# Turning the leading expert's second half of tokens ahead of the branch, with one raw buffer for the wide weights

## The chip, the cores and the metric

One core of one Trainium2 chip runs the whole kernel in one launch. The metric is the device time of that core in microseconds, as the median over several executions. Single executions of this kernel lie within about 0.3% of one another.

## The reference

Three stages follow one another; all is float32 but for `moe2`'s weights, which arrive as 64-bit floats.

```python
# attention: B, H, S, D = 4, 8, 768, 48, step by step over S
cur = einsum('bhd,bhe->bhde', u[None] * kt, vt)
y[:, :, t] = einsum('bhd,bhde->bhe', rt, state + cur)
state = wt[..., None] * state + einsum('bhd,bhe->bhde', kt, vt)
# x: 3072 tokens of 384; top-1 of 8 experts by cosine similarity
logits = xn @ en.T / tau
expert_idx = argmax(logits, axis=1); gate_w = softmax(logits)[chosen]
out[mask] = gate_w * (maximum(x[mask] @ w1[e], 0) @ w2[e])      # w1 384x1024, w2 1024x384
# wide stage on all tokens
h = maximum(maximum(x @ w1, x @ w2), x @ w3)                    # 384x768 each
return h @ w_out                                                # 768x384
```

## The kernel before

**Precision by halves.** Each matrix product of the last two stages is made of three single passes: a value is split into a high part (rounded to the matmul format) and a low part (the value minus the high one), and high x high, low x high and high x low are summed in PSUM. So every tile of weights or activations costs one copy (ScalarE, makes `hi`) and one subtraction (VectorE or GpSimd, makes `lo`).

**Attention and routing (span 0 to about 199 us).** The sequence is cut into 24 chunks of 128 tokens. Each chunk's outputs go to DRAM (`xs_d`), its logits feed the routing, which yields for each expert the list of its tokens. The expert with most tokens is known early. For it, called the leading expert or expert 0 here, the first 256 tokens (`EARLY`) are gathered, turned by TensorE (`early_x`, L851 on), split, and multiplied by `w1` in eight calls `early_h`, one per 128 columns of `w1`, all before the routing's last numbers are known. `early_lo` makes the low halves on VectorE. The gathers of its third and fourth quarter are issued on GpSimd after the last routing step, but nothing uses them before the branch.

**The branch.** The final counts of the experts choose one of three copies of the expert code, with different tile widths (`CAPS`). Every engine loads two numbers (`over`, L92) into registers and takes the branch (L100) for itself, when its own queue has come so far. In the profiled execution the copy with `CAPS[0]` runs, in which expert 0 has 432 columns.

**The experts (to about 419 us).** `experts()` (L1025 on) is a list written out by hand: all work is issued in program order (`manual_schedule`), and each engine takes its own instructions in that order, waiting by semaphores. It starts with `expert_x(0, 1)`, which turns and splits the gathered third and fourth quarter, and four matmuls on a constant tile (`IDLE[1]`), whose results nobody reads. Then 64 steps follow, eight per expert. Step s does `expert_h` of step s (9 matmuls), `expert_y` of step s-2 (9 matmuls), the copies and subtractions for coming weights, and their loads on SyncE. For expert 0, `expert_h` covers only columns 256 to 432.

**The wide weights.** 24 tiles of 128x384 of 64-bit words become hi and lo parts by integer steps on VectorE, in three stages (`wide_weights`, L940 on): stage 0 allocates a raw tile (`raw64`, two buffers) and issues its transfer of 384 KB on SyncE; stage 1 is four VectorE operations and the ScalarE copy that makes hi; stage 2 is four VectorE operations that make lo. In stage 1, the first operation (L960) reads the high words out of the raw tile, the fourth (L964) reads them again. In stage 2, L970 writes a scratch tile `t2`, L971 reads the low words and `t2`, L972 reads `t2` and writes lo. Tiles 0 to 17 are spread over the expert steps, tile i being loaded at step 2+3i, and its stages 1 and 2 done at steps 3+3i and 4+3i. Tiles 18 to 23, the six of `w_out`, are done in the wide stage.

**The wide stage (to the end).** Six blocks of 512 tokens; each has six `wide_h` (27 matmuls of 512 columns, then two maxima on VectorE, L999 and L1000, a copy on ScalarE and a subtraction on GpSimd, L1007) and four `wide_out` (18 matmuls each, L1017). The `wide_out` of block j run behind the first `wide_h` of block j+1. In block 0, each `wide_h` is followed in program order by stages 1 and 2 of one `w_out` tile, and the transfer of the tile after next; after the second `wide_h` VectorE also splits the next block's activations (`split_y`). The first `wide_out` needs all six `w_out` tiles, the last of them for its last three matmuls.

Of the kernel before, what the change touches and what calls it, by code (L numbers as in the profile page):

```python
# [20 lines left out]
DM = H * D  # L21
# [3 lines left out]
P = 128  # L25
# [11 lines left out]
IDLE = 4, 4  # L37
# [9 lines left out]
class Block:  # L47
# [6 lines left out]
    def run(self):  # L54
        tc, nc = self.tc, self.nc
        with ExitStack() as es:
# [8 lines left out]
                         for t in ("hw1", "lw1", "hw2", "lw2")}  # L65
            self.ring["raw"] = [ring.tile([P, 384], F32, name=f"raw_{i}") for i in range(RAW)]
# [45 lines left out]
    def attention(self):  # L112
# [3 lines left out]
        with ExitStack() as es:  # L116
# [97 lines left out]
            en = cp.tile([E, DM], F32, name="en")  # L214

            def setup2():
                ess = cp.tile([E, 1], F32, name="ess")
                enn = cp.tile([E, 1], F32, name="enn")
                act.activation(out=en, in_=emb, func=AF.Square, accum_out=ess)
# [6 lines left out]
                dve.tensor_scalar(out=en, in0=emb, scalar1=enn, scalar2=self.rtau[:E], op0=ALU.mult, op1=ALU.mult)  # L226
                dve.tensor_copy(enp[:, :, :D], en.rearrange("p (h d) -> p h d", h=H))
# [5 lines left out]
            def setup2b():  # L233
# [4 lines left out]
                for d in range(3):  # L238
                    pe.transpose(tq[:, d * E:(d + 1) * E], en[:, d * P:(d + 1) * P], ident[:E, :E])
# [357 lines left out]
            with tc.manual_schedule():  # L597
# [132 lines left out]
                for f in range(4, 8):  # L730
                    head(f)
                for n, op in enumerate(order()):
                    op()
                    if n == 0:
                        self.early_lo(2, early[2])
                offsets()
                for f in range(3, 8):
                    self.early_lo(f, early[f])

# [112 lines left out]
    def early_x(self, q, t):  # L852
# [4 lines left out]
        tv = t[:, :3 * P].rearrange("p (d t) -> p d t", d=3)  # L857
        two = lambda z: z.rearrange("p (d t) -> p d t", t=EARLY)
# [49 lines left out]
    def expert_h(self, e, f, c0=0):  # L908
        cap = self.caps[e]
        wh, wl = self.w1s[e, f]  # L910
        xh, xl = self.xT[e]
        t = self.ptile("h", 2)
        n = 0
        for a, b in ((wh, xh), (wl, xh), (wh, xl)):
            for d in range(3):
                self.pe.matmul(t[:, c0:cap], a[:, d, :], b[:, d, c0:], start=(n == 0), stop=(n == 8))  # L916
# [23 lines left out]
    def wide_weights(self, i, stage):  # L940
# [11 lines left out]
        if stage == 0:  # L952
            self.raws[0, i] = self.work.tile([P, 384], U64, tag="raw64", name="raw64")
# [13 lines left out]
        else:  # L967
            t1, t2 = self.wide, self.work.tile([P, 384], U32, tag="t1", name="t1", bufs=1)
# [57 lines left out]
    def experts(self):  # L1026
# [11 lines left out]
        with tc.manual_schedule():  # L1038
            self.dve.memset(self.gsort, 0.0)
            if early:  # L1040
                self.expert_x(0, 1)
                t = self.ptile("y", 3)
                for _ in range(IDLE[1]):
                    self.pe.matmul(t, self.warm[:, :P], self.warm, start=True, stop=True)
            else:
# [54 lines left out]
            for i in range(WIDE, WIDE + 2):  # L1100
                self.wide_weights(i, 0)
            k, pend = 0, None
            for j in range(6):
                hs, nxt = [], None
                for f in range(6):
# [6 lines left out]
                    if j == 0:  # L1112
                        for stage in 1, 2:
                            self.wide_weights(WIDE + f, stage)
                        if WIDE + f + 2 < 24:
                            self.wide_weights(WIDE + f + 2, 0)
# [164 lines left out]
```

## Time and profile before

| | |
|---|---|
| three timed runs | 735.00, 736.92, 737.33 us; median 736.92 |
| the profiled execution | 733.96 us; span of its instructions 732.2 us |
| busy: TensorE, VectorE, ScalarE, GpSimd | 708.7, 428.2, 306.8, 257.0 us |
| mean granted TensorE clock | 0.992 of full |
| DMA | 69.05 MB, 94 GB/s on average |

The span runs from the first to the last instruction of one execution; all times below are microseconds from its start. PE is TensorE's matmul side, PEld its weight loads, PEldq its sequencer; DVE is VectorE, ACT ScalarE, POOL GpSimd, SPq the queue of SyncE. `L916` is line 916 of the kernel before. Names of tiles stand without their numbers, `out<-in`; a name such as `mh` or `hw` can stand for another use of the same storage.

### The profile page before, as it was taken

The page shows a single profiled execution, that of the slowest core. Times are in us where ns is not written, and L with a number is a line of the kernel's source. Part 1 is how long each engine was busy: PE and PEld are TensorE (multiplying, and loading weights), DVE is VectorE, ACT ScalarE, POOL GpSimd, SP SyncE. Part 2 cuts the span into 40 slices and gives each one's busy share as a digit, 9 for nine tenths or more (in the row PEclk, how much of TensorE's full clock was granted, in tenths as well). Part 3 has the DMA queues.
Part 4 walks back from the last instruction along what each step waited for, and adds up shares of the span by engine and source line. Part 5 has one row for each costly group of instructions (what it writes and reads, how often), then busy time and mean ns, then how long its engine had stood idle before and what let it go on. Part 6 is the DMA issues. An engine that isn't in the chain of part 4 may idle for free.

```text
span 732.2 us, 13468 instructions
## 1 busy us (share of the span) xinstructions
PE 708.7 (97%) x4861; PEld 627.6 (86%) x4861; DVE 428.2 (58%) x938; ACT 306.8 (42%) x720; POOL 257.0 (35%) x271
## 2 busy tenths in 40 slices
PE   7999999999799999999999999999999999999994
PEld 4788888888789999999999988988988988889884
DVE  7889999998747986878788368431032031221110
ACT  4667666765445554555556322222121221221120
POOL 6857657476531401201100023343333333223122
PEclk9999999999999999999999999999999999999998
DMA  9997878753365537656554111000100100000001
GB/s 154 171 149 139 138 135 138 144 89 118 104 186 165 170 115 216 202 152 195 152 173 147 60 29 59 23 22 1 44 1 0 44 1 11 33 1 21 22 2 46
DMA packets 146444, 69.05 MB, mean 94 GB/s; under 512 B 104967, under 2 KB 140931, under 8 KB 146360
## 3 DMA queue, kind: packets, MB, share of 16 engines
q1 hardware_dynamic: 141752, 58.27, 35.1%
q0 software_dynamic: 4032, 9.74, 4.2%
q8 instruction: 42, 0.69, 0.4%
q14 instruction: 42, 0.34, 0.1%
q10 hardware_dynamic: 576, 0.01, 0.1%
HBM read 58.52 MB, written 9.48 MB: 93 GB/s over the span
## 4 chain that ended last, share of the span: by engine, by line
PE 85%; DVE 7%; issue 3%; DMA 2%; ACT 1%; POOL 1%; SPq 0%; POOLq 0%; DVEq 0%; ACTq 0%
PE psy L993 16%; PE psT L993 15%; PE psy L933 13%; PE psh L916 13%; PE psh L1017 9%; PE psT L275 4%; PE psA L356 3%; PE psM L426 3%; PE psY L417 3%; PE psY L410 2%; PE psM L384 1%; DMA out_dram<-raw,idx 1%; DVE es L337 1%; PE psM L294 1%; DVE gs L324 1%
## 5 line engine op out<-in xcount | busy, mean ns | idle before, releaser
L999 DVE TENSOR_TENSOR xg<-psT,xg 128x512 f32<-128x512 f32 x18 | 12.4, 690 | 112.8 <-PE psT L993 80.8
L827 DVE TENSOR_TENSOR lw<-raw,hw 128x384 fp32r<-128x384 f32 x120 | 62.3, 553 | 15.8 <-ACT hw L825 14.0
L825 ACT ACTIVATE hw<-raw 128x384 fp32r<-128x384 f32 x123 | 60.7, 524 | 17.7 <-ACT hw L825 10.2
L1007 POOL TENSOR_TENSOR lw<-xg,hw 128x512 fp32r<-128x512 f32 x24 | 31.5, 1311 | 100.4 <-ACT hw L1006 100.4
L841 POOL DMA_INDIRECT xg<-xs_d,idxs x25 | 26.8, 1073 | 111.0 <-PE psT L903 44.6
L1007 POOL TENSOR_TENSOR lh<-xg,hh 128x512 fp32r<-128x512 f32 x12 | 16.1, 1340 | 115.1 <-ACT hh L1006 115.1
L309 POOL TENSOR_SCALAR_AFFINE_SELECT AT<-c 128x1024 f32<-128x1024 f32 x24 | 38.9, 1619 | 49.0 <-ACT c L304 48.9
L1006 ACT ACTIVATE hw<-xg 128x512 fp32r<-128x512 f32 x24 | 15.2, 635 | 97.0 <-DVE xg L1000 97.0
L993 PE MATMUL psy<-yh,mh 128*128 128x512 f32 x162 | 46.7, 396 | 0.2 <-ACT ys L937 0.2
L993 PE MATMUL psy<-yl,mh 128*128 128x512 f32 x162 | 46.6, 395 | 0.0
L993 PE MATMUL psT<-yh,ml 128*128 128x512 f32 x162 | 46.6, 396 | 0.0
L993 PE MATMUL psy<-yh,ml 128*128 128x512 f32 x162 | 46.5, 396 | 0.0
L993 PE MATMUL psT<-yl,mh 128*128 128x512 f32 x162 | 46.5, 396 | 0.0
L993 PE MATMUL psT<-yh,mh 128*128 128x512 f32 x162 | 46.5, 395 | 0.0
L922 DVE SCALAR_TENSOR_TENSOR lh<-psh,hh 128x420 fp32r<-128x420 f32 (+6 forms) x56 | 31.4, 561 | 19.8 <-ACT hh L921 19.5
L916 PE MATMUL psh<-xh,hw 128*128 128x420 f32 (+7 forms) x177 | 42.0, 345 | 0.3 <-DVE lh L922 0.3
L916 PE MATMUL psh<-xh,lw 128*128 128x420 f32 (+7 forms) x183 | 42.0, 339 | 0.0
L1033 POOL DMA_INDIRECT out_dram<-raw,idx x24 | 23.7, 987 | 49.5 <-ACT raw L1023 32.5
L916 PE MATMUL psh<-xl,hw 128*128 128x420 f32 (+7 forms) x177 | 40.7, 337 | 0.0
L933 PE MATMUL psy<-hh,hw 128*128 128x420 f32 (+6 forms) x168 | 40.1, 344 | 0.0
L933 PE MATMUL psy<-lh,hw 128*128 128x420 f32 (+6 forms) x168 | 39.2, 341 | 0.0
L933 PE MATMUL psy<-hh,lw 128*128 128x420 f32 (+6 forms) x168 | 39.2, 341 | 0.0
(329 smaller groups left out, 1801.7 us busy)
## 6 DMA issues: line engine op xcount, KB each, us to landing
raw<-in_moe_w_dram SPq DMA_DIRECT2D x128, 192.0 KB
raw<-in_moe_w_dram SPq DMA_DIRECT2D x18, 384.0 KB
wb<-in_w_dram SPq DMA_DIRECT2D x24, 192.0 KB
kb<-in_k_dram SPq DMA_DIRECT2D x24, 192.0 KB
rb<-in_r_dram SPq DMA_DIRECT2D x24, 192.0 KB
vb<-in_v_dram SPq DMA_DIRECT2D x24, 192.0 KB
xs_d<-xt SPq DMA_DIRECT2D x24, 192.0 KB
raw<-in_moe_w_out_dram SPq DMA_DIRECT2D x6, 384.0 KB
```

What stands on the lines that cost most here:

```text
L275: pe.transpose(t[:112, p * P:(p + 1) * P], flat(src)[:, p * P:p * P + 112], ident)
L309: pool.affine_select(out=x["AT"].rearrange("s q p t -> s (q p) t"), in_=x["c"].rearrange("t q p -> t (q p)").unsqueeze(2).to_broadcast([P, ...
L825: self.act.activation(out=hi, in_=raw, func=AF.Copy)
L827: eng.tensor_tensor(out=lo, in0=raw, in1=hi.bitcast(F32), op=ALU.subtract)
L841: self.pool.indirect_dma_start(out=t[:n], out_offset=None, in_=self.xs_d[0:rows], in_offset=bass.IndirectOffsetOnAxis(ap=self.idxs[:n, 4 * ...
L916: self.pe.matmul(t[:, c0:cap], a[:, d, :], b[:, d, c0:], start=(n == 0), stop=(n == 8))
L922: self.dve.scalar_tensor_tensor(out=lo, in0=t[:, c0:cap], scalar=0.0, in1=hi.bitcast(F32), op0=ALU.max, op1=ALU.subtract)
L933: self.pe.matmul(self.yb[m][:, :cap], a[:, m, :], b, start=(f == 0 and n == 0), stop=(f == 7 and n == 2))
L993: self.pe.matmul(t, a[:, d, f * P:(f + 1) * P], b[:, d, :], start=(n == 0), stop=(n == 8))
L1007: self.pool.tensor_tensor(out=lo, in0=c2, in1=hi.bitcast(F32), op=ALU.subtract)
L1017: self.pe.matmul(t[:, :DM], a[:, c], b[:, f, :], start=(n == 0), stop=(n == 17))
L1033: self.pool.indirect_dma_start(out=self.out, out_offset=bass.IndirectOffsetOnAxis(ap=self.idx2[:, k:k + 1], axis=0), in_=o, in_offset=None ...
```

## The change

The third and fourth quarter of expert 0's tokens are turned by `early_x` behind the last `early_h`, still in the attention part, into a pair of tiles of their own (`x1`); ScalarE copies the high part at once, and VectorE's two subtractions come behind the last `early_lo`. `expert_h` of expert 0 reads that pair. `expert_x(0, 1)` and the four matmuls on the constant tile behind the branch go. The room for `x1` comes from three places: `raw64` has one buffer instead of two, stage 2 writes its scratch over the raw tile's high words, and a scratch tile of the setup goes (its two users write `emb` and another scratch tile). With one raw buffer a tile's transfer can only be issued once the tile before has gone through stage 2, and in block 0 of the wide stage the transfers are issued one tile ahead instead of two.

```diff
-IDLE = 4, 4
...
+            self.x1 = [ring.tile([P, 3, 512 - EARLY], F32R, name=f"x1{t}") for t in "hl"]
...
-            en = cp.tile([E, DM], F32, name="en")
...
-                act.activation(out=en, in_=emb, func=AF.Square, accum_out=ess)
+                act.activation(out=rp.tile([P, DM], BF16, tag="jq", name="jq")[:E], in_=emb, func=AF.Square, accum_out=ess)
...
                 for f in range(4, 8):
                     head(f)
+                rest = [self.early_x(q, bank("M", 3)) for q in (2, 3)]
                 for n, op in enumerate(order()):
                     op()
...
                 for f in range(3, 8):
                     self.early_lo(f, early[f])
+                for low in rest:
+                    low()
...
         tv = t[:, :3 * P].rearrange("p (d t) -> p d t", d=3)
+        if q > 1:
+            hi, lo = (z[:, :, (q - 2) * P:(q - 1) * P] for z in self.x1)
+            self.act.activation(out=hi, in_=tv, func=AF.Copy)
+            return lambda: self.dve.tensor_tensor(out=lo, in0=tv, in1=hi.bitcast(F32), op=ALU.subtract)
...
-        xh, xl = self.xT[e]
+        xh, xl = self.x1 if c0 else self.xT[e]
...
-                self.pe.matmul(t[:, c0:cap], a[:, d, :], b[:, d, c0:], start=(n == 0), stop=(n == 8))
+                self.pe.matmul(t[:, c0:cap], a[:, d, :], b[:, d, :cap - c0], start=(n == 0), stop=(n == 8))
...
-            self.raws[0, i] = self.work.tile([P, 384], U64, tag="raw64", name="raw64")
+            self.raws[0, i] = self.work.tile([P, 384], U64, tag="raw64", name="raw64", bufs=1)
...
-            t1, t2 = self.wide, self.work.tile([P, 384], U32, tag="t1", name="t1", bufs=1)
+            t1, t2 = self.wide, high
...
-            if early:
-                self.expert_x(0, 1)
-                t = self.ptile("y", 3)
-                for _ in range(IDLE[1]):
-                    self.pe.matmul(t, self.warm[:, :P], self.warm, start=True, stop=True)
-            else:
+            if not early:
...
-            for i in range(WIDE, WIDE + 2):
-                self.wide_weights(i, 0)
+            self.wide_weights(WIDE, 0)
...
-                        if WIDE + f + 2 < 24:
-                            self.wide_weights(WIDE + f + 2, 0)
+                        if WIDE + f + 1 < 24:
+                            self.wide_weights(WIDE + f + 1, 0)
```

## Rows read from the trace of the kernel before

**Rows 1.** The page's chain that ended last, share of the span by engine.

```profile
PE 85%; DVE 7%; issue 3%; DMA 2%; ACT 1%; POOL 1%; SPq 0%; POOLq 0%; DVEq 0%; ACTq 0%
```

**Rows 2.** Timeline of TensorE around the branch: start, us, operation, count, [idle before].

```profile
198.16 0.28 PE L876 MATMUL psT<-ml,mh 128*128 128x256 f32 x1
201.22 1.36 PE L903 MATMUL psT<-ident,hw 128*128 128x128 f32 x6 [2.78 <-issue]
202.51 1.89 PE L1044 MATMUL psy<-warm 128*128 128x512 bf16 x4
203.84 1.34 PE L916 MATMUL psh<-xh,lw 128*128 128x176 f32 x6
...
207.72 0.79 PE L933 MATMUL psy<-mh,hw 128*128 128x432 f32 x3
```

**Rows 3.** Waits from 424 to 470: us in total, times, longest.

```profile
PEld psh L1017 <- DVE ol L972: 0.2, 1, 0.2
```

**Rows 4.** Chain of waits from 180 to 240: start, us, what.

```profile
215.56 0.66 PE psT L903 x6
...
228.82 1.74 PE psh L916 x9
```

**Rows 5.** Lines 92, 100 and 108 on TensorE's sequencer: ns min/median/max, first and last start.

```profile
L92 PEldq TENSOR_LOAD <-over x2: 312/400/488, 196.1 to 196.7; - x2
...
L100 PEldq COMPARE_BRANCH  x1: 3797/3797/3797, 197.2 to 197.2; - x1
...
L108 PEldq COMPARE_BRANCH  x1: 3786/3786/3786, 719.3 to 719.3; - x1
```

**Rows 6.** Timeline of GpSimd from 184 to 214: the fourth quarter's gather.

```profile
195.02 1.00 POOL L841 DMA_INDIRECT hw<-xs_d,idxs  x1 [0.30 <-issue]
```

**Rows 7.** DMA issues from 186 to 210: count, median us from issue to landing.

```profile
hw<-xs_d,idxs POOLq DMA_INDIRECT x2, 3.1
```

**Rows 8.** Stretches: us, PE, PEld, DVE, ACT, POOL busy, PEclk, DMA share, GB/s.

```profile
201.00:201.25 0.25, 0.03 (x1) 0.06 (x1) 0.00 (x0) 0.00 (x0) 0.00 (x0) 0.80 0.58 80
...
204.50:204.75 0.25, 0.25 (x4) 0.25 (x4) 0.25 (x1) 0.00 (x0) 0.00 (x0) 0.87 0.77 297
```

**Rows 9.** Timeline of VectorE from 212 to 262: two wide tiles and a low half.

```profile
220.06 0.56 DVE L972 SCALAR_TENSOR_TENSOR ml<-t,t 128x384 fp32r<-128x384 f32 x1
...
223.69 0.35 DVE L960 TENSOR_SCALAR t<-raw 128x384 uint32<-128x384 uint32 x1
...
226.22 0.34 DVE L922 SCALAR_TENSOR_TENSOR ml<-psh,ml 128x176 fp32r<-128x176 f32 x1 [0.80 <-ACT ml L921]
```

**Rows 10.** Timeline of SyncE's queue from 430.5: four transfers of w_out, merged.

```profile
431.38 21.75 SPq L954 DMA_DIRECT2D raw<-in_moe_w_out_dram  x4
```

**Rows 11.** The stretch in which the first of these transfers ends, columns as in rows 8.

```profile
433.75:434.00 0.25, 0.25 (x3) 0.21 (x2) 0.24 (x1) 0.25 (x1) 0.00 (x0) 1.00 0.19 62
```

**Rows 12.** Timeline of VectorE from 420 to 475: tiles 18, 19 and 23.

```profile
431.39 0.56 DVE L972 SCALAR_TENSOR_TENSOR ol<-t,t 128x384 fp32r<-128x384 f32 x1
...
433.25 0.35 DVE L960 TENSOR_SCALAR t<-raw 128x384 uint32<-128x384 uint32 x1
...
434.42 1.55 DVE L964 SCALAR_TENSOR_TENSOR t<-raw,t 128x384 uint32<-128x384 uint32 x1
...
465.90 0.56 DVE L972 SCALAR_TENSOR_TENSOR ol<-t,t 128x384 fp32r<-128x384 f32 x1
```

**Rows 13.** Timeline of GpSimd from 424 to 475: one low half of wide_h.

```profile
434.13 1.42 POOL L1007 TENSOR_TENSOR lh<-xg,hh 128x512 fp32r<-128x512 f32 x1 [3.79 <-ACT hh L1006]
```

**Rows 14.** Line 964, all 24: ns min/median/max, first and last start.

```profile
L964 DVE SCALAR_TENSOR_TENSOR t<-raw,t x24: 557/559/1552, 215.4 to 462.4; 128x384 uint32<-128x384 uint32 x24
```

**Rows 15.** Timelines of GpSimd and VectorE from 184 to 214, then line 495 as a whole.

```profile
183.76 3.09 POOL L827 TENSOR_TENSOR lw<-raw,hw 128x384 fp32r<-128x384 f32 x3
...
184.97 1.92 DVE L495 TENSOR_SCALAR pay<-i,aa,tid 128x32 fp32r<-128x32 f32 x2
...
L495 DVE TENSOR_SCALAR pay<-i,aa,tid x24: 289/292/1039, 57.9 to 192.3; 128x32 fp32r<-128x32 f32 x24
```

More of the change, by code (lines that the diff above doesn't have):

```diff
@@ L225, in setup2 @@
                 dve.reciprocal(out=enn, in_=enn)
-                dve.tensor_scalar(out=en, in0=emb, scalar1=enn, scalar2=self.rtau[:E], op0=ALU.mult, op1=ALU.mult)
-                dve.tensor_copy(enp[:, :, :D], en.rearrange("p (h d) -> p h d", h=H))
+                dve.tensor_scalar(out=emb, in0=emb, scalar1=enn, scalar2=self.rtau[:E], op0=ALU.mult, op1=ALU.mult)
+                dve.tensor_copy(enp[:, :, :D], emb.rearrange("p (h d) -> p h d", h=H))
                 pool.memset(neg1, -1.0)
@@ L238, in setup2b @@
                 for d in range(3):
-                    pe.transpose(tq[:, d * E:(d + 1) * E], en[:, d * P:(d + 1) * P], ident[:E, :E])
+                    pe.transpose(tq[:, d * E:(d + 1) * E], emb[:, d * P:(d + 1) * P], ident[:E, :E])
                 for q, o in ((0, 0), (1, 64)):
```

## The prediction

> **What bounds the kernel now.** I read the page first, and of it the chain that ended last: TensorE holds 85% of it, every other engine 7% or less [rows 1]. So an edit is worth what it moves on TensorE's queue, and elsewhere only where TensorE waits. Two places in the timelines matter for this change. The first is the branch between attention and experts: TensorE's last early matmul starts at 198.16 and takes 0.28, the next instruction starts at 201.22; then come six transposes, four filling matmuls from 202.51, the first `expert_h` at 203.84, and the first `expert_y` at 207.72 [rows 2]. The reader is to see 9.3 us between 198.44 and 207.72, of which the 27 `expert_h` matmuls need about 3 at the full clock. The second place is the last half of the trace, the view of waits from 424 to 470: TensorE's first `wide_out` waits 0.2 us for `ol`, the last split wide weight, from VectorE [rows 3]. That is small, and it says that VectorE has no time to spare there: whatever comes later on VectorE in the first wide block arrives on the chain.
>
> **The branch.** Before it the change adds, on TensorE, two times three transposes behind `head(7)`. Six transposes at the full clock took 0.66 us [rows 4], so TensorE ends near 199.1 instead of 198.44. After it the change removes the same transposes, which ran slowly there, 201.22 to 202.51, and the four fillers, 202.51 to 203.84: together 2.62 us of queue [rows 2]. ScalarE's two copies and VectorE's two subtractions also move ahead; the wait of the third group of `expert_h` for `xl` goes.
>
> But the transposes bring a wait with them. TensorE's sequencer runs ahead of its array: it loaded the branch's registers at 196.1, while the array worked until 198.44, and branched at 197.2; the branch took 3.80 us and the later one at the end of the kernel 3.79 [rows 5], though that one stands with other work around it, so I take 3.8 as a fixed price that starts when the sequencer gets there. Behind the waiting transposes the sequencer gets there later. The gather of the fourth quarter was issued at 195.02 [rows 6] and gathers of that tile land 3.1 us after their issue [rows 7], at 198.1. Queued behind that wait are the register loads and the branch: 198.1, plus 1.1 from the register loads to the branch, plus 3.8, plus the 0.2 between 201.0 and 201.22, gives the first `expert_h` at 203.2 instead of 203.84. So of 2.62 us removed, 2.0 return as a later branch.
>
> Then the clock. After the array had stood since 198.44 the granted clock fell from full to one half in the stretch 201.00 to 201.25 (0.80 in it), 2.4 to 1.2 GHz, and it rose again in the stretch 204.50 to 204.75 (0.87) [rows 8], with work going on since 201.22. Before, the transposes and fillers spent most of that slow stretch; after, there is nothing but `expert_h` to spend it. I take one as long, 3.3 us from the first instruction. Six `expert_h` matmuls took 203.84 to about 205.1 with half of it at the low clock, later ones 0.11 each (9 in about 1 us); at the low clock twice that, 0.22. From 203.2 on, the slow stretch holds 15 of the 27 matmuls, the other 12 take 1.35: the first `expert_y` starts at 207.9 against 207.72. **The branch is worth +0.2 us.** Its bounds: no fall of the clock, 203.2 + 3.0 = 206.2, is -1.5; an instruction load that is held up by the weight transfers that SyncE starts meanwhile, taken at one more microsecond, is +1.2. I take +0.2, since the stop of the array gets longer than the one that let the clock fall before (199.1 to 203.2, against 198.44 to 201.22).
>
> ScalarE and VectorE also reach their branches later, by about the two copies and subtractions. VectorE's next due work is the split of the first `w2` tile and the first `lh`, wanted by `expert_y` at 207.9; I cost it at nothing.
>
> **One raw buffer in the expert phase.** With one buffer the transfer of wide tile i+1 must wait for the last step on tile i, where it ran ahead before. The tightest shape is the first: last step ends at 220.06 + 0.56 = 220.62, the next tile's first step starts at 223.69 [rows 9], a gap of 3.1 us, and a lone 384 KB transfer takes 2.6 (below). With `w1` and `w2` transfers beside it I allow a stall of 1 us on VectorE. Behind it stands `lh`, which ended at 226.56; TensorE wants that PSUM buffer back at 228.82 [rows 4, 9], 2.3 us later. SyncE's loads behind the waiting transfer are wanted two steps on. Cost zero; with 2.3 us of cover gone it would cost what exceeds it. Stage 2's `t2`, now in place, writes every other word instead of a dense tile; no row shows such a write, so I bound it by the fast and the slow rate of steps of that size, 0.35 (the first step) and 0.56 (the last step) [rows 9], between 0 and 0.2 us each; I take 0, because the step that reads every other word runs at the fast rate as well.
>
> **One raw buffer in the first wide block.** Here six tiles are split in a row, one for each `wide_h`, and VectorE has no pause. Before, tile 20's transfer was issued at 431.38 [rows 10], as soon as tile 18 had been read, and tile 19 was there already. After, tile 19's transfer can only be issued when tile 18's last step ends, 431.39 + 0.56 = 431.95. The transfer issued at 431.38 had moved its bytes by about 434.0, the stretch where the rate falls to 62 GB/s [rows 11]: 2.6 us. So tile 19 lands near 434.55. VectorE wants it at 433.25 [rows 12], after the two maxima: a stall of 1.3 us at least.
>
> It hits a second thing. GpSimd's `lh` subtraction runs from 434.13 to 435.55 [rows 13], at a fixed distance from the maxima. Before, the fast steps were through when it began and only the fourth step, 1.55 us instead of the usual 0.56, met it [rows 12, 14]. After, the first step itself would begin at 434.55 in the middle of it. Does a single-input step wait for GpSimd? A `tensor_scalar` pair on VectorE that began at 184.97 ended at 186.89, with GpSimd's three subtractions ending at 186.85, at up to 1.04 each where the median is 0.29 [rows 15]. I take it that it waits: first step from 435.55, fourth step 1.17 later (434.42 - 433.25), 0.56 long: done at 437.2 instead of 435.97. With the start of a held step overlapped, **1.1 us for each stalled tile**; without being held, 434.55 + 1.17 + 0.56 = 436.3, 0.3 us.
>
> The Trainium skill, SBUF — State Buffer, section "Who interferes with whom", says the same more sharply: `tensor_scalar` in a 2-port mode and GpSimd exclude each other for a whole instruction, and whoever issues first goes first. The trace agrees in the pair of [rows 15]; by that rule the stall is the 1.1, without it 0.3, and it speaks against the change.
>
> Tiles 19, 21, 22 and 23 stall; at tile 20 VectorE has the three wide subtractions of `split_y` to do meanwhile, and the transfer is hidden. Four times 1.1 is 4.4. The last step on tile 23 ended at 465.90 + 0.56 = 466.46 [rows 12], and TensorE waited for just that [rows 3]; it would end at 470.9. PSUM is not late before that: `wide_h` has two sets of banks, so the maxima may lag by more than a whole block of 27 matmuls. **The wide block is worth +4.4 us** (0 if all were hidden, 1.2 with 0.3 a tile, 6.1 if the clock also falls in the 4 us pause and costs half of a slow stretch, 1.7).
>
> **Sum.** Against its own execution, 733.96 us (span 732.2 and 1.8 around it): +0.2 + 4.4 = +4.6, 738.6. That execution lies 3.0 us under the median of the three runs, 736.92; on the median the forecast is **741.5 us**.
>
> **Rivals.** (1) The single-input steps run beside GpSimd: the fourth step, begun after GpSimd's end, is no longer held, and 1.0 us of the wait is paid back. The stall is 0.3 a tile, the sum 0.2 + 1.2: 738.3. This is the rival of the other side, not slower by anything that can be told. It decides as soon as a tile costs under 0.5 us (4 x 0.5 + 0.2 = 2.2). For it: no row shows exactly these steps held. Against it: the pair of [rows 15]. 20%. (2) The clock falls in the pause before the last `wide_out` weights: 4.6 + 1.7, 743.2. For it: a stop of 2.8 us let it fall at the branch. Against it: a matmul stands between the waits for `oh` and `ol`. 20%. (3) The sequencer is not held by the transposes' wait (branch at 197.2 as before): 27 matmuls from 201.22, 4.7 us with the slow stretch, to 205.9, so -1.8 at the branch and +2.6 in all, 739.5. Against it: in the trace the sequencer takes its instructions in order, waits included. 8%. (4) The wide tiles are hidden after all, because a transfer behind an idle queue lands sooner than the one measured, and only the branch counts, between -1.5 and +1.2: near 737.1. Against it: tile 19 has 1.3 us for 2.6. 10%. My forecast: 42%.
>
> **Numbers.** A change under 0.3%, 2.2 us, can hardly be told from none. Slower by more: the forecast, rival 2 and about half of rival 3, 0.67. No difference: rival 1, the other half of 3, and rival 4 but for its lower end, 0.28. Faster: 0.05, rivals 3 and 4 together (-1.8) and what I have not seen. The range runs from 737.4 (between rivals 4 and 1) to 744.4 (rival 2 and a microsecond for a late branch).
>
> **What would show it.** In the changed profile: the branch on TensorE starting near 199.2 and `expert_h` near 203.2; a clock at one half over its first 15 matmuls; `expert_y` near 207.9; VectorE idle before the first step of tiles 19, 21, 22 and 23, released by a transfer; the fourth step back at 0.56; TensorE waiting about 4 us at the last weights of the first `wide_out`. The prediction is wrong if that wait is under 2 us, if the branch starts at 197.2, or if the expert phase shows TensorE waiting for `lh`.

## The result and the profile after

The changed kernel took 744.02 us (median of four runs, 743.65 to 744.63) against 736.14 for the kernel before in the same comparison, 7.9 us more. The ratio is 1.0118, with a 95% interval of [1.0088, 1.0147]; it is an estimate of its own and not the quotient of the two medians (1.0107). The direction and the places were forecast; the size was not: 4.6 us were forecast on a base of 736.92, where the ratio gives 8.7 us and 745.6, above the range's end of 744.4. Between the two profiled executions lie 9.7 us (743.65, span 741.7, against 733.96, span 732.2). The profiled execution of before lies 2.2 us under its kernel's median, that of after 0.4 under its own, so the profiles show some 1.8 us more than the medians do. Single executions scatter by more than the 0.3% of the first section: 29 of the kernel before, timed beside four of the experiments, took 731.83 to 740.42 us, at mean granted clocks from 0.994 down to 0.981 and one at 0.934, so a profile shows one draw of several. Line numbers of the part discussed are five higher than before: `L921` to `L1022` are `L916` to `L1017` there.

The chain that ended last, share of the span by engine. The reader is to compare it with [rows 1]: VectorE went from 7% to 12% and DMA from 2% to 5%, so the chain now runs for a while through transfers and the steps behind them.

```profile
PE 76%; DVE 12%; DMA 5%; issue 3%; ACT 2%; POOL 1%; SPq 0%; POOLq 0%; ACTq 0%; DVEq 0%
```

Cut at the same five points of TensorE's timeline, the two spans differ as follows (us; each number a difference of two starts or ends in the profile).

| stretch | before | after | difference |
|---|---|---|---|
| start to the end of the last early matmul | 198.44 | 197.79 | -0.65 |
| from there to the first `expert_y` | 9.28 | 11.02 | +1.74 |
| from there to the first `wide_h` | 211.79 | 214.07 | +2.28 |
| first wide block, to the first `wide_h` behind its `wide_out` | 56.89 | 63.32 | +6.43 |
| from there to the end | 255.8 | 255.5 | -0.3 |

**The branch.** TensorE's timeline, columns as in [rows 2]: the last early matmul, the transposes now ahead of the branch, the first nine matmuls of `expert_h`, the first `expert_y`.

```profile
197.51 0.28 PE L881 MATMUL psT<-ml,mh 128*128 128x256 f32 x1
197.63 0.99 PE L857 MATMUL psM<-ident,hw 128*128 128x128 f32 x6
203.00 1.53 PE L921 MATMUL psh<-x1h,lw 128*128 128x176 f32 x6 [4.37 <-issue]
204.33 0.84 PE L921 MATMUL psh<-x1l,lw 128*128 128x176 f32 x3
...
208.81 1.26 PE L938 MATMUL psy<-mh,hw 128*128 128x432 f32 x3
```

Then lines 92 and 100 on TensorE's sequencer, columns as in [rows 5]; below them, the two stretches in which the granted clock falls to one half (2.4 to 1.2 GHz) and comes back, columns as in [rows 8].

```profile
L92 PEldq TENSOR_LOAD <-over x2: 313/402/490, 198.1 to 198.7; - x2
...
L100 PEldq COMPARE_BRANCH  x1: 3637/3637/3637, 199.1 to 199.1; - x1
```

```profile
203.00:203.25 0.25, 0.25 (x1) 0.25 (x2) 0.00 (x0) 0.08 (x1) 0.00 (x0) 0.54 0.97 363
...
209.75:210.00 0.25, 0.25 (x3) 0.25 (x2) 0.00 (x0) 0.17 (x1) 0.25 (x1) 0.81 0.87 160
```

The reader is to see that the branch starts at 199.1, two microseconds later than in [rows 5], that `expert_h` starts at 203.00, and that the slow stretch lasts from 203.0 to 209.85, 6.8 us, where [rows 8] have 3.4. All 27 matmuls of `expert_h` lie in it.

**The first wide block.** VectorE's timeline, columns as in [rows 12]: the end of tile 18, then tile 19's first step, fourth step and in-place write, and the last step of tile 23. Below it, the one operation of GpSimd that stands in the way, as in [rows 13].

```profile
434.79 0.56 DVE L977 SCALAR_TENSOR_TENSOR ol<-raw,t 128x384 fp32r<-128x384 f32 x1
...
438.25 0.79 DVE L965 TENSOR_SCALAR t<-raw 128x384 uint32<-128x384 uint32 x1 [1.52 <-DMA raw<-in_moe_w_out_dram]
...
439.87 0.56 DVE L969 SCALAR_TENSOR_TENSOR t<-raw,t 128x384 uint32<-128x384 uint32 x1
...
441.29 0.36 DVE L975 TENSOR_SCALAR raw<-raw 128x384 uint32<-128x384 uint32 x1
...
473.06 0.56 DVE L977 SCALAR_TENSOR_TENSOR ol<-raw,t 128x384 fp32r<-128x384 f32 x1
```

```profile
437.53 1.30 POOL L1012 TENSOR_TENSOR lh<-xg,hh 128x512 fp32r<-128x512 f32 x1 [3.79 <-ACT hh L1011]
```

The transfer is released when tile 18's last step ends, 435.35, and wakes VectorE at 438.25. The first step then takes 0.79 where it took 0.35 [rows 12], and ends at 439.04, just behind GpSimd's operation (438.83); the fourth step is back at 0.56 from 1.55. The view of waits from 420 to 490 counts the same thing four times:

```profile
DVE t L965 <- DMA raw<-in_moe_w_out_dram: 6.1, 4, 1.6
```

What TensorE makes of it: its timeline at the last two weights of the first `wide_out`, and the stretches in which its clock falls and comes back there.

```profile
471.82 0.44 PE L1022 MATMUL psh<-oh,hw 128*128 128x384 f32 x1 [1.90 <-ACT oh L970]
...
473.68 0.69 PE L1022 MATMUL psh<-ol,hw 128*128 128x384 f32 x1 [1.42 <-DVE ol L977]
```

```profile
472.62:472.87 0.25, 0.00 (x0) 0.00 (x0) 0.25 (x1) 0.00 (x0) 0.00 (x0) 0.61 0.00 0
...
479.37:479.62 0.25, 0.25 (x3) 0.25 (x2) 0.00 (x0) 0.00 (x0) 0.00 (x0) 0.74 0.08 25
```

The wait of 0.2 us [rows 3] has become two waits, 1.9 and 1.4, and the pause let the clock fall to one half for 6.8 us.

**The experts.** TensorE's waits between 208 and 423, the largest two:

```profile
PE psy L938 <- ACT ys L942: 1.0, 3, 0.5
PE psh L921 <- DVE lh L927: 0.7, 1, 0.7
```

The first is new: the view of before has no such wait at `expert_y`. ScalarE's copy of an expert's result (`ys`) comes late at three borders between experts. Compared step by step, TensorE falls behind there by 0.48, 0.57 and 0.46 us, 1.5 in all; another 0.4 is lost near 285, at the second wait, which other kernels without one raw buffer show too (below). How `ys` comes to be late can be read at the first border, on VectorE and then on ScalarE:

```profile
291.37 0.36 DVE L965 TENSOR_SCALAR t<-raw 128x384 uint32<-128x384 uint32 x1 [0.41 <-DMA raw<-in_moe_w_dram]
...
293.15 0.52 ACT L970 ACTIVATE mh<-t 128x384 fp32r<-128x384 f32 x1 [3.46 <-DVE t L969]
...
293.96 1.30 ACT L942 ACTIVATE ys<-psy 128x408 f32 x3
```

VectorE waits 0.41 us for the wide tile's transfer (0.56 at the second border; in the kernel before it waits at neither), ScalarE's copy `mh` of that tile waits for VectorE's fourth step, and `ys` stands behind `mh` in ScalarE's queue. At the third border `ys` waits for another operation of VectorE (`yl`).

### The profile page after: what moved, and what is told of

Same layout as the page of the kernel before. It is cut to its first block, busy times and chain, and to the rows that moved or that the text cites. A ratio compares the mean times of both kernels' runs of the same rounds, so it can differ in the third digit from the quotient of the medians.

```text
span 741.7 us, 13465 instructions
## 1 busy us (share of the span) xinstructions
PE 711.4 (96%) x4857; PEld 630.2 (85%) x4857; DVE 426.7 (58%) x938; ACT 306.5 (41%) x720; POOL 254.7 (34%) x271
## 4 chain that ended last, share of the span: by engine, by line
PE 76%; DVE 12%; DMA 5%; issue 3%; ACT 2%; POOL 1%; SPq 0%; POOLq 0%; ACTq 0%; DVEq 0%
PE psy L998 13%; PE psy L938 12%; PE psT L998 12%; PE psh L921 11%; PE psh L1022 8%; PE psT L273 4%; PE psA L354 3%; PE psM L424 3%; PE psY L415 2%; PE psY L408 2%; DMA raw<-in_moe_w_out_dram 2%; DMA hw<-xs_d,idxs 1%; PE psM L382 1%; DMA raw<-in_moe_w_dram 1%; PE psT L908 1%
## 5 line engine op out<-in xcount | busy, mean ns | idle before, releaser
L921 PE MATMUL psh<-xh,hw 128*128 128x420 f32 (+6 forms) x168 | 40.6, 349 | 0.7 <-DVE lh L927 0.7
L921 PE MATMUL psh<-xl,hw 128*128 128x420 f32 (+6 forms) x168 | 39.2, 341 | 0.0
L921 PE MATMUL psh<-xh,lw 128*128 128x420 f32 (+6 forms) x168 | 39.2, 341 | 0.0
```

Source lines behind the costliest of these rows:

```text
L921: self.pe.matmul(t[:, c0:cap], a[:, d, :], b[:, d, :cap - c0], start=(n == 0), stop=(n == 8))
```

## The experiments

The theory after these profiles: the wide block is late through the one raw buffer alone, by a stall and by the clock that falls in the pause; the branch is late because the four filling matmuls are gone and the slow stretch lasts twice as long. Its rivals: the sequencer's wait costs the branch its time, the fillers being worthless; the parts hurt only together; and the stall's microseconds are all there is in the wide block. Ratios are to the kernel before, timed on the same one of three chips, and as above they are not the quotients of the medians shown; one execution of each kernel is profiled.

### The one raw buffer alone

The kernel before, with one buffer for the raw tiles and `t2` in place.

```diff
-            ... tag="raw64", name="raw64")
+            ... tag="raw64", name="raw64", bufs=1)
...
-            t1, t2 = self.wide, self.work.tile([P, 384], U32, tag="t1", name="t1", bufs=1)
+            t1, t2 = self.wide, high
...
-            for i in range(WIDE, WIDE + 2):
-                self.wide_weights(i, 0)
+            self.wide_weights(WIDE, 0)
...
-                            self.wide_weights(WIDE + f + 2, 0)
+                            self.wide_weights(WIDE + f + 1, 0)
```

> The kernel before with the raw-buffer part of the change alone: one raw buffer, transfers of the w_out tiles one ahead, t2 written in place; the branch is as before. Theory A (late transfers in block 0 of the wide stage hold VectorE, TensorE waits for the last w_out weights and its clock falls; a smaller loss of 1.9 us at the borders of experts): 7 to 9 us slower than before, 743 to 745, with a wait of some 4 us at the first wide_out. Rival B (the early turn is what costs, by moving ScalarE and VectorE late): within 2 us of before.

Measured: 742.28 against 734.83 us, 1.0088 [1.0053, 1.0122]. The first wide block took 63.18 us, as in the changed kernel (63.32); the branch took 9.19 from the last early matmul to `expert_y`, as before (9.28). TensorE's waits from 208 to 490:

```profile
PE psh L1017 <- ACT oh L965: 2.2, 1, 2.2
PE psy L933 <- ACT ys L937: 1.8, 3, 1.0
PE psh L1017 <- DVE ol L972: 1.2, 1, 1.2
```

All three waits of the changed kernel are here without the early turn: the pause at the last `w_out` tile, and the three late `ys`. So the one buffer brings most of the loss: 0.88% of 1.18% by the ratios, 7.45 us of 7.88 by the medians.

### The early turn alone

The changed kernel with two raw buffers. The room comes from elsewhere: the third buffers of `hh` and `lh` lie in `x1`, which is free by then.

```diff
+            for t, x in zip(("hh", "lh"), self.x1):
+                self.ring[t] = [self.cw.tile([P, 512], F32R, name=f"{t}_{i}") for i in range(2)] + [flat(x)[:, :512]]
...
-            self.hT[e, f] = [self.work.tile([P, 512], F32R, tag=t, name=t, bufs=3)[:, :cap] for t in ("hh", "lh")]
+            self.hT[e, f] = [self.take(t)[:, :cap] for t in ("hh", "lh")]
...
-            ... tag="raw64", name="raw64", bufs=1)
+            ... tag="raw64", name="raw64", bufs=2)
...
-            self.wide_weights(WIDE, 0)
+            for i in range(WIDE, WIDE + 2):
+                self.wide_weights(i, 0)
...
-                            self.wide_weights(WIDE + f + 1, 0)
+                            self.wide_weights(WIDE + f + 2, 0)
```

> The changed kernel with two raw buffers again and w_out transfers two ahead (room from the third hh and lh buffers, which move into x1 once expert 0 is through); the early turn stays, t2 stays in place. Theory A: the wait at the first wide_out is back under 0.3 us and the borders of experts cost nothing; what is left is the branch, between -1 and +2 us against before, 735 to 738. Rival B: still 5 us or more slower than before. Rival C (writing t2 in place is slow): VectorE's in-place step over 0.5 us and some of the loss stays.

Measured: 737.12 us, 1.0026 [1.0005, 1.0048]. The wide block is back at 56.77. The branch took 11.40; the slow stretch ran from 201.57 to 211.8, 10.2 us. The sequencer, TensorE's waits in the expert phase, and what stands ahead of the longest of them on VectorE:

```profile
L94 PEldq TENSOR_LOAD <-over x2: 312/402/492, 199.1 to 199.7; - x2
...
L102 PEldq COMPARE_BRANCH  x1: 3897/3897/3897, 200.1 to 200.1; - x1
```

```profile
PE psh L923 <- DVE x1l L929: 2.8, 1, 2.8
...
PE psy L1000 <- ACT ys L944: 0.2, 1, 0.2
```

```profile
285.29 0.36 DVE L967 TENSOR_SCALAR t<-raw 128x384 uint32<-128x384 uint32 x1 [4.36 <-DMA raw<-in_moe_w_dram]
```

The waits for `ys` at the expert borders are gone (the one left is at the first `wide_h`, and before has it too). The wait near 285 is here with two buffers, and longer, so it doesn't belong to the one buffer. VectorE waits there for a wide tile's transfer, 1.97 us in the kernel before, 1.7 to 2.7 in most other profiles, and 4.1 to 4.4 in two: this one, and the one with 14 fillers ahead and 4 behind. Others with the same expert code are not among the two, so some 2.5 us of this profile may be chance; they are neither the branch's nor the one buffer's. The early turn by itself loses 0.26%, and 0.88% + 0.26% = 1.14% agrees with the 1.18% of the whole change: each part costs by itself, and within the intervals, 0.2 to 0.35% each way, the parts add up.

### One raw buffer for the experts, two for the wide stage

As the last, but tiles 0 to 17 share one buffer.

```diff
-            self.raws[0, i] = self.work.tile([P, 384], U64, tag="raw64", name="raw64", bufs=2)
+            t = "raw64" if i % 2 and i >= WIDE else "raw"
+            self.raws[0, i] = self.work.tile([P, 384], U64, tag=t, name=t, bufs=1)
```

> The changed kernel with one raw buffer for tiles 0 to 17 and two, two ahead, for the six w_out tiles. Theory A: the wide block's 6.4 us come back and the 1.9 us at the borders of experts stay: about 738 to 740. If the expert phase alone makes VectorE late into the wide stage, less than 4 us come back.

Measured: 737.37 us, 1.0034 [1.0014, 1.0055]; wide block 56.75. TensorE's waits in the expert phase:

```profile
PE psy L940 <- ACT ys L944: 1.0, 3, 0.6
PE psh L923 <- DVE x1l L929: 0.9, 1, 0.9
```

The three late `ys` follow the one buffer into this kernel, and their wait is the changed kernel's 1.0 us. In the times, 1.0034 against 1.0026 doesn't resolve them, and the time lies under the 738 to 740 us expected. Nearly all that the one buffer costs, it costs in the wide stage.

### No filling matmuls, the early turn left out

The kernel before without its four matmuls behind the branch, nothing else changed.

```diff
-IDLE = 4, 4
+IDLE = 4, 0
```

> The kernel before without its four filling matmuls behind the branch, nothing else changed. If they shorten the slow stretch of the clock (3.4 us with them, 6.8 us in the changed kernel without), 0.5 to 2 us slower than before although 1.3 us of work is gone. If the stretch does not depend on them, up to 1.3 us faster.

Measured: 737.52 us, 1.0024 [1.0000, 1.0048]. The clock's stretches and TensorE's timeline:

```profile
201.75:202.00 0.25, 0.00 (x0) 0.00 (x0) 0.00 (x0) 0.25 (x2) 0.00 (x0) 0.87 0.73 178
...
212.00:212.25 0.25, 0.25 (x2) 0.23 (x1) 0.00 (x0) 0.00 (x0) 0.00 (x0) 0.65 0.64 234
```

```profile
202.29 1.58 PE L916 MATMUL psh<-xh,lw 128*128 128x176 f32 x6 [0.91 <-ACT xh L905]
204.48 0.95 PE L916 MATMUL psh<-xl,lw 128*128 128x176 f32 x3 [0.61 <-DVE xl L906]
...
209.07 1.35 PE L933 MATMUL psy<-mh,hw 128*128 128x432 f32 x3
```

The last early matmul ended at 197.75. Counted from there, `expert_h` starts 0.9 us sooner than in [rows 2] (4.54 against 5.40), but its group that waits for `xl` only 0.1 sooner (6.73 against 6.85): in this kernel the fillers stood largely in a wait. `expert_y` starts 2.0 later (11.32 against 9.28): in this profile the slow stretch lasts 10.2 us instead of 3.4. The prediction had booked the fillers' removal as a gain; a loss is what the time shows, though its interval reaches down to none.

### The early turn with the four fillers kept

The early turn with two raw buffers, and the four matmuls behind the branch put back.

```diff
+            if early:
+                t = self.ptile("y", 3)
+                for _ in range(4):
+                    self.pe.matmul(t, self.warm[:, :P], self.warm, start=True, stop=True)
...
```

> As the run with the early turn alone, and the four filling matmuls behind the branch kept. Theory E (without the fillers it is expert_h itself that runs through the slow stretch, and the stretch gets longer for it): the slow clock ends some 3.4 us after the first instruction as before, and it is 0.5 to 2 us faster than the early turn alone although it has 1.3 us more to do. Rival: the slow stretch is as long as without them, and it is 0.5 to 1.3 us slower.

Measured: 735.29 us, 1.0016 [0.9995, 1.0037]. The clock's stretches:

```profile
203.00:203.25 0.25, 0.25 (x2) 0.05 (x2) 0.00 (x0) 0.00 (x0) 0.00 (x0) 0.52 1.24 338
...
206.25:206.50 0.25, 0.25 (x3) 0.25 (x3) 0.00 (x0) 0.00 (x0) 0.00 (x0) 0.66 0.65 240
```

With the fillers the slow stretch is 3.4 us, as long as before. In time the step from 1.0026 is within the intervals. `expert_y` starts 10.79 after the last early matmul instead of 11.40: the fillers themselves take 1.24 us (202.92 to 204.16) of what the shorter stretch gives back. The early turn doesn't pay even so; the sequencer's wait remains.

### The wait for the gather taken away

The early turn with two raw buffers; the transposes of the third and fourth quarter read the identity instead of the gathered rows, so this kernel leaves these tokens out.

```diff
-            self.pe.transpose(t[:, d * P:(d + 1) * P], g[:, d * P:(d + 1) * P], self.ident)
+            self.pe.transpose(t[:, d * P:(d + 1) * P], self.ident if q > 1 else g[:, d * P:(d + 1) * P], self.ident)
```

> As the run with the early turn alone, but the six early transposes read the constant identity tile instead of the gathered rows (so expert 0's third and fourth quarter are not computed): they wait for no transfer. Theory A (the sequencer takes its queue in order, so the wait for the fourth quarter's gather holds the branch): the branch on TensorE starts near 197.2 as before, some 2 us sooner than in the run with the early turn alone, and the first expert_h starts near 201.2; 2 us or more faster than that run. Rival (the branch waits for the array to finish, or is held by its own instruction load): the branch or its end stays where it was, within 0.5 us, and so does the time.

Measured: 733.72 us, 0.9984 [0.9967, 1.0002]; 8.30 us from the last early matmul to `expert_y`, and no fall of the clock there (this profile has a slow stretch earlier, from 187.75 to 191.5). The sequencer, then TensorE:

```profile
L94 PEldq TENSOR_LOAD <-over x2: 312/400/488, 197.6 to 198.1; - x2
...
L102 PEldq COMPARE_BRANCH  x1: 3357/3357/3357, 198.6 to 198.6; - x1
```

```profile
198.97 0.82 PE L859 MATMUL psM<-ident 128*128 128x128 f32 x6
202.19 0.88 PE L923 MATMUL psh<-x1h,lw 128*128 128x176 f32 x6 [2.40 <-issue]
...
206.35 0.57 PE L923 MATMUL psh<-x1h,hw 128*128 128x176 f32 x3 [1.94 <-DVE mh L929]
```

The register loads come 1.5 us before the last early matmul ends (199.13), where with the wait they come 0.4 after it (199.1 against 198.72). So the gather holds the sequencer by 1.9 us. That the fall of the clock goes with it is seen in this one profile: the array stands for 2.40 us instead of 4.63. In time, the wait and what hangs on it are worth 0.42% (1.0026 to 0.9984, each against the kernel before on its own chip), more than the early turn's whole loss. So the rival holds as far as it says that the sequencer's wait costs the branch its time; whether the fillers are worthless isn't settled by the times (1.0016 with them, 1.0026 without). The last row shows what limits the branch next: TensorE waits 1.94 us for VectorE, whose first operation behind its own, later branch (201.4) starts at 205.39. The prediction had put VectorE's later branch at nothing.

### Filling matmuls ahead of the branch

Matmuls on the constant tile right behind the early transposes, ahead of the branch, so that the array works while the sequencer branches. 14, 18 and 24 of them with the early turn and two raw buffers; 14 with the four behind the branch as well; and 14 in the kernel before, in place of its four.

```diff
                 rest = [self.early_x(q, bank("M", 3)) for q in (2, 3)]
+                idle(14)
```

> As the run with the early turn alone, and 14 matmuls of 512 columns on the constant tile behind the early transposes, ahead of the branch: the sequencer runs ahead to the branch while the array works on them for some 3 us. If the array's stop behind the branch is what lets the clock fall (theory A), the clock stays full and expert_h runs at 0.11 us each from about 203: 2 to 3.5 us faster than the run with the early turn alone, near 733 to 735. Rival D (the sequencer cannot run that far ahead, or the clock falls all the same): the branch comes later by up to 3 us and nothing is gained.

> As the run with 14 filling matmuls ahead of the branch, with 18. If the array may not stop for long, a little better than 14: 732 to 733.5. With 24 the sequencer's register loads came 2.0 us later than with 14; if 18 already hold it, 0.5 to 1 us slower than with 14.

> As the run with 14 matmuls ahead of the branch, with 24 of them, 5 us of work. Theory A (the array's stop lets the clock fall): no stop of more than 1 us is left, the clock stays full in every execution, and it is 1 to 3 us faster than with 14, near 731 to 732. Rival D (the sequencer cannot run that far ahead): its register loads come 2 us later than with 14, and it is slower than with 14.

> The early turn alone with 14 filling matmuls ahead of the branch and four behind it. If the gain of the run with 14 ahead is the clock's, and four behind shorten a slow stretch where it still comes, this is as fast as that run or up to 1 us faster, 732.5 to 733.5 where before is at 734.8; if the four only take their time, 0.9 us slower than that run.

> The kernel before with its four filling matmuls behind the branch replaced by 14 ahead of it, behind the last early_h; nothing is turned early. If the gain of the run with 14 fillers comes from the clock alone, this has it as well: the transposes behind the branch run at the full clock, 0.66 us instead of 1.3, and the time is 1.5 to 3 us under before. If the early turn is needed for it, within 1 us of before.

| kernel | us | ratio | last early matmul to `expert_y` | slow stretch behind the branch |
|---|---|---|---|---|
| turn, 14 ahead | 733.45 | 0.9973 [0.9953, 0.9993] | 12.47 | 6.8 |
| turn, 18 ahead | 733.89 | 0.9983 [0.9960, 1.0006] | 9.10 | none |
| turn, 24 ahead | 733.84 | 1.0003 [0.9985, 1.0022] | 10.14 | none |
| turn, 14 ahead, 4 behind | 734.74 | 0.9988 [0.9965, 1.0011] | 9.02 | none |
| before, 14 ahead for 4 behind | 736.59 | 1.0029 [1.0009, 1.0049] | 11.61 | 10.2 |

For comparison, the kernel before has 9.28 and 3.4, the early turn alone 11.40 and 10.2.

TensorE and its sequencer with 14, then with 24:

```profile
198.75 3.18 PE L183 MATMUL psY<-warm 128*128 128x512 bf16 x14
204.85 1.38 PE L924 MATMUL psh<-x1h,lw 128*128 128x176 f32 x6 [2.92 <-DVE gsort L1047]
```

```profile
L94 PEldq TENSOR_LOAD <-over x2: 313/400/487, 200.4 to 201.0; - x2
```

```profile
199.13 5.34 PE L183 MATMUL psY<-warm 128*128 128x512 bf16 x24
205.45 0.88 PE L924 MATMUL psh<-x1h,lw 128*128 128x176 f32 x6 [0.97 <-DVE lw L831]
```

With 24 the clock holds there, but the register loads come at 200.4, 2.0 us behind the end of the last early matmul (198.43), where with 14 they come 0.4 behind it (198.4 and 198.04): a microsecond and a half goes to the later branch, and the 731 to 732 us expected didn't come. (The engines in the brackets aren't what `expert_h` waited for in these rows: TensorE's branch itself ended at 204.6 with 14 and at 205.2 with 24.)

14 is the one number whose interval lies below 1: 733.45 against 734.83, and 0.995 of the early turn without them (737.12), on the same chip. It is the one version whose time is clear of the kernel before, by 0.3%; it is also the best of several tried, and 18 can't be told from it. Why it gains isn't shown by its own profile: that execution took 735.8 us, among the longer of its twelve (730.12 to 736.08), has a slow stretch of 6.8 us, and needs the longest of all for the branch, whose instruction took 4.98 us on TensorE's sequencer; with four more fillers behind the branch, and the same program up to it, it took 3.40.

A rival for part of the gain stands untested. All kernels with the turn and two raw buffers also keep the third `hh` and `lh` buffers elsewhere. In the four of them without a slow stretch or a long wait in the expert phase (18 and 24 ahead, four behind, no wait), the time from the first `expert_y` to the first `wide_h` is 210.84 to 211.00 us, against 211.79 in the kernel before: 0.8 to 0.9 us that neither the turn nor the fillers are shown to give. The turn's own loss may be larger than 0.26% by as much.

In the kernel before, the same 14 lose 0.29%, which its expectation had on neither side. There they make the sequencer late: its register loads come 0.6 us ahead of the end of the last early matmul (199.21), where without them they came 2.3 ahead of it (196.1 and 198.44, [rows 5] and [rows 2]); behind the early turn, whose gather holds the sequencer anyway, 14 cost nothing of this kind. And the clock fell although the array stood for little:

```profile
L92 PEldq TENSOR_LOAD <-over x2: 313/400/488, 198.6 to 199.2; - x2
...
199.05 3.19 PE L181 MATMUL psY<-warm 128*128 128x512 bf16 x14
203.47 0.83 PE L904 MATMUL psT<-ident,hw 128*128 128x128 f32 x6 [1.22 <-issue]
204.96 1.59 PE L917 MATMUL psh<-xh,lw 128*128 128x176 f32 x6 [0.65 <-ACT xh L906]
```

### Filling matmuls in the wide pause

The changed kernel, with 16 matmuls on the constant tile ahead of the last `w_out` tile's in the first `wide_out`.

```diff
+            if f == 5:
+                for _ in range(fill):
+                    self.pe.matmul(idle, self.warm[:, :P], self.warm, start=True, stop=True)
```

> The changed kernel with 16 matmuls on the constant tile ahead of the last w_out tile's products in the first wide_out, 3.4 us of work in the place where TensorE waits 3.8. If the 6.4 us that the first wide block loses are 3.8 of waiting and 2.6 of slow clock behind it, the clock stays full there and 2 to 2.6 us come back against the changed kernel: about 741.5, 0.9% over before. If the clock costs nothing there, or falls for another reason, the time is that of the changed kernel within 1 us, 1.1 to 1.2% over before.

Measured: 743.53 against 735.71 us, 1.0102 [1.0072, 1.0133]; the first wide block took 60.69 us instead of 63.32, at the full clock. TensorE:

```profile
473.41 3.63 PE L1024 MATMUL psh<-warm 128*128 128x512 bf16 x16
477.38 0.45 PE L1026 MATMUL psh<-ol,hw 128*128 128x384 f32 x1 [0.16 <-DVE ol L977]
```

In the block 2.6 us come back, and 3.8 stay: the first is the price of the clock, the second that of the stall. In the times the gain isn't resolved (1.0102 against 1.0118), and the whole of this execution, 744.57 us, doesn't show it either: its branch has a slow stretch of 10.2 us, where the changed kernel's profile has 6.8.

## Why the prediction was wrong in size, step by step

**The branch, +0.2 forecast, +1.74 measured, and some 0.4 more in the slow rest behind `expert_y`.** The sequencer's step was right: behind the transposes' wait the register loads came at 198.1, the branch at 199.1 (199.2 forecast), `expert_h` at 203.00 (203.2); without the wait it all comes 1.9 us sooner against the array. That it fits to 0.2 us is in part luck: the part ahead ran 0.65 shorter, and the gather took 3.7 us from its issue (194.37) to the transposes that wait for it (198.08), where 3.1 was put. What failed is "I take one as long, 3.3 us from the first instruction". The slow stretch was 6.8 us, and 6.8 or 10.2 in six other kernels without the fillers behind the branch; with the four fillers behind the branch, it was 3.4 in all three profiles in which the clock fell. The profiles agree on this, one for each kernel; the times don't resolve it. Nor is it the whole of it: stretches of 3.4 us also stand elsewhere with no filler in them, from 187.75 in two profiles and from 283.9, behind a wait of 2.5 us, in one. Then all 27 matmuls of `expert_h`, not 15, cost 0.21 to 0.22 each, and `expert_y` came at 208.81 instead of 207.9. The fillers were booked as 1.33 us of queue gone; with them taken out alone, the time rises by 0.24% (0.00 to 0.48%). The loss of the early turn alone, 0.26%, is 1.9 us on the clock of the runs, above the upper bound of +1.2: that bound had a late instruction load in it, and no longer slow stretch (the branch's own length varies from 3.36 to 4.98 us over the profiles; no run shows that an instruction load does it). Its profile, though, has the long wait near 285 besides the branch.

**The first wide block, +4.4 forecast, +6.43 measured.** The mechanism stands: stalls at tiles 19, 21, 22 and 23 and none at 20; the transfer wakes VectorE 2.9 us after the release (2.6 forecast); the held first step; the fourth step freed; `t2` in place at no cost (0.36 at L975, the fast rate). The stall of a tile measured 0.94 us (7.47 from tile to tile instead of 6.53) against 1.1: 1.5 of waiting and 0.44 of a held first step, less 0.98 at the fourth. The four make 3.8. Rival 1, no hold, falls with the 0.79 at L965. The forecast's queue of work was right, and the clock was not: the sum has it at nothing in the pause. Rival 2, given 20%, came true, and cost 2.6 us where half a slow stretch of 3.3, 1.7, was put down, because this stretch lasted 6.8 too. "A matmul stands between the waits" was no protection.

Of the rule of the Trainium skill, SBUF — State Buffer, section "Who interferes with whom", the trace bears out the direction: a `tensor_scalar` that meets GpSimd ends behind it. By a full exclusion it would have ended at 438.83 + 0.35 = 439.18; it ended at 439.04, 0.21 behind GpSimd's end, as at the other three stalled tiles (0.21 to 0.22), and GpSimd's spans are rough.

**The experts, 0 forecast, about 1.5 measured in the profile.** "TensorE wants that PSUM buffer back 2.3 us later" covered `lh` in one shape of step and overlooked another customer: at the border of two experts TensorE waits for ScalarE's `ys`, which has no such slack. Three borders lose 0.5 us each. The late transfer gets there through ScalarE's queue, in which `ys` stands behind a copy that waits for the wide tile. All four kernels with one raw buffer for the experts show three such waits (1.0 to 1.8 us); with two buffers, no profile shows more than one, of 0.4 at most. The times don't resolve the sum. The prediction's own sign for this part, TensorE waiting for `lh`, did appear (0.7 near 285), but the kernel before has it too (0.3), and two buffers show 0.2 to 2.8.

**The sum.** Of the 5 us between 4.6 and the profile's 9.7, about 2 are the branch's, 2 the wide block's, 1.9 the experts'; the early part ran 0.65 shorter, which no step of the change explains: the profile of the kernel before has a slow stretch of 3.4 us near 10 us, the changed kernel's has none. The branch's 2 come from the length of a slow stretch that was carried over from a place where the fillers ran in it to one where they don't; the wide block's come from a slow stretch that the sum left out (2.6), less a stall sized too large (3.8 for 4.4). The runs bear the split out: 0.88% (6.5 us; 7.45 by the medians) with one raw buffer alone, where 4.4 were forecast, and 0.26% (1.9 us) with the turn alone, where 0.2 were.

**Left open.** Why a slow stretch lasts 3.4, 6.8 or 10.2 us; why the clock fell with 14 fillers in the kernel before and in the one profile of the best version; what an execution of that version in its faster half looks like (its six faster ones ran at mean granted clocks of 0.988 to 0.997, the six slower ones at 0.986 to 0.990); what the place of the `hh` and `lh` buffers is worth.

## What to carry to other kernels

A stop of TensorE can cost the slow stretch behind it besides the stop, and a stretch read at one place, with other work in it, is no price for another: here the profiles showed it two and three times as long once the filling matmuls were out of it. Before taking filling matmuls out, try that alone. An instruction queued ahead of a branch puts its wait in front of the branch, so work moved there must have its data sooner, or bring matmuls that keep the array busy meanwhile. When a buffer is taken for room, look at the place where its tiles follow one another without a pause; and look first for a tile that is dead by then, as `x1` was here for `hh` and `lh`.

## What the runs showed of the hardware

The branch took TensorE's sequencer between 3.36 us (without the gather's wait) and 4.98 us (14 fillers ahead; 3.40 in another kernel with the same program up to it). On ScalarE its record is 0.05 us long, but ScalarE's first operation behind it starts 4.6 us later with 14 fillers ahead (199.6 and 204.19), and 3.9 later in the changed kernel (199.3 and 203.17). In ten profiles the clock fell at the branch, in two in the wide pause; elsewhere there were slow stretches near 10 us in eleven profiles, at 187.75 in two and at 283.9 in one. But for the kernel's end, every stretch came out near 3.4, 6.8 or 10.2 us. At the branch the clock fell behind stops of 1.22 and 0.65 us (14 fillers in the kernel before), and in another kernel held behind one of 2.40 (no wait for the gather). TensorE's sequencer did its register loads 2.3 us before the array's last early matmul ended in the kernel before, and 0.3 us behind that end in the changed kernel, where a wait for a gather stood in front of them. Behind the early turn, 14 and 18 filling matmuls left them where the gather had put them (0.4 to 0.5 us behind that end); 24 made them 1.6 us later.
